# Attention values with the exponentials as stationary operand, a ones column for the sums, and a turn by TensorE

## Chip, cores, metric

One core of one Trainium2 chip. The metric is the device time of one execution in microseconds, lower is better.

## The reference, cut to what matters

Attention over 8 batches, 8 heads, 576 queries, 16 beacon keys and 576 causal keys, head size 64, followed by a gated feed-forward block (512 to 1536 to 512) on the 4608 tokens.

```python
k_all = np.concatenate([beacon_k, k], axis=2)          # 592 keys
v_all = np.concatenate([beacon_v, v], axis=2)
scores = scale * q @ k_all.T                           # causal mask on the 576
a = np.exp(scores - max); a /= a.sum(-1) + 1e-9
x = (a @ v_all) -> (B*S, H*D)
out = (gelu(x @ w_gate) * (x @ w_val)) @ w_out
# ... cut
```

## The kernel before

Heads are worked in pairs (four pairs per batch), keys in five tiles t of up to 128. Scores are computed as keys by queries, so the exponentials expT have keys on partitions. Only the causal part is computed: it is packed in four chunks. Each chunk has its scores in one of **two** PSUM buffers (`psum_s`), from which ScalarE takes the exponential into `expT`; GpSimd (in batch 0 VectorE) masks the diagonal afterwards.

```python
CHUNK_W = [512, 480, 464, 208]           # columns of a chunk, for each of two heads
psum_s = tile_pool(name="psum_s", bufs=2, space=PSUM)    # scores, gate/value: 2 x 2 banks
psum_x = tile_pool(name="psum_x", bufs=1, space=PSUM)    # x and sums: 3 banks
psum_o = tile_pool(name="psum_o", bufs=1, space=PSUM)    # output matmuls: 1 bank

def scores(b, m, c):
    s_ps = psum_s.tile([P, 2, 512], FP32, tag="s")
    ...                                   # matmuls of 64 rows, two heads side by side
    act(expT[:, :, o : o + w], s_ps[:, :, 0:w], ACT.Exp, scale=QK_SCALE)
    if b: masks(b, m, c)

def attend(b, m, t, wide=False):          # V or ones stationary, expT moving
    for w, (ps, base, split) in enumerate(x_of[i]):       # w = 0: x, w = 1: the sums
        for q0, q1 in ((S_LO[t], split), (max(split, S_LO[t]), S)):
            for hi in range(2):           # two heads in two 64-column tiles of TensorE
                mm(ps[64*hi : 64*hi+64, base+q0 : base+q1],
                   ones[0:kr, :] if w else v_sb[0:kr, t, 2*m+hi, :],
                   expT[0:kr, hi, e0 : e0 + q1 - q0], ...)

def normalize(b, m, ...):                 # ... cut: the sums stand in all 64 partitions
    act(x_sb, x_ps, ACT.Copy)
    nc.vector.transpose(zT_sb, z_ps)
    nc.vector.reciprocal(r_sb, ...)       # 18 values after the 32x32 transpose
    nc.vector.transpose(rec_sb, r_sb broadcast)
    nc.vector.tensor_tensor(out=xT_sb[...], in0=x_sb, in1=rec_sb, op=mult)
```

In batches 1 to 7 the output matmuls of the previous batch, `o(n)`, are spread between the pairs. `ab` computes two chunks, `cd` the other two, `av` is attend and normalize:

```python
o(6); ab(0); o(10); cd(0); o(8)
for m in range(1, NPAIR):
    ab(m); av(m - 1); cd(m); o(6 if m < NPAIR - 1 else 5)
av(3, direct=True); o(7)
# then 12 x gate_val(b, fi): 8 matmuls of 512 columns each
```

Batch 0 has no previous batch and runs its value matmuls at the end of its attention.

The softmax here doesn't subtract the row's maximum and nothing guards it: scores larger than these inputs give would overflow.

## Time and profile before

| | before |
|---|---|
| median time | 398.38 us (397.85 to 398.61), 398.12 with the fourth run |
| span of the profiled run | 396.2 us |
| TensorE, ScalarE, VectorE busy | 97%, 51%, 48% |
| length of a batch (first scores to first scores of the next) | 42.18 us |
| distance of two pairs within a batch | 4.03 us |

The groups below, from the list of costliest groups, are those that the change removes (line, engine, operation, tile names, shapes, count | busy us, mean ns | idle before).

```profile
L155 PE MATMUL x_ps<-expT,ones 128*64 128x432 bf16 (+1 forms) x558 | 41.2, 243 | 0.0
L304 DVE STREAM_TRANSPOSE zT_sb<-x_ps 128x576 f32<-128x576 f32 x29 | 22.7, 781 | 29.9 <-ACT x_sb L158 29.9
L307 DVE STREAM_TRANSPOSE rec_sb<-r_sb 128x576 f32<-128x576 f32 x29 | 22.6, 778 | 1.0
```

Busy time of TensorE here counts pipelined matmuls one over the other, so 41.2 us of the ones matmuls isn't 41.2 us of span, and "busy" also covers short waits.

### The profile page before, as it was taken

What the parts mean: (1) busy time and instruction counts of PE and PEld (TensorE: products, weight loads), DVE (VectorE), ACT (ScalarE), POOL (GpSimd) and SP (SyncE); (2) the same over time, 40 slices, a digit from 0 to 9 for tenths busy, and PEclk for the clock granted to TensorE, in tenths of its full rate; (3) what the DMA queues carried; (4) which work ended last, traced back from release to release, by engine and by line L of the source; (5) the groups of instructions that cost most, each with busy time, mean ns of one, the idle gap of its engine ahead of it and who ended that gap; (6) DMA issues with size and microseconds to landing.
All of it is one profiled execution on the core that took longest, in us unless ns stands there. A gap on an engine that the chain in (4) does not pass through costs nothing.

```text
span 396.2 us, 7413 instructions
## 1 busy us (share of the span) xinstructions
PE 382.3 (97%) x3046; PEld 185.9 (47%) x3046; DVE 190.5 (48%) x304; ACT 202.2 (51%) x280; POOL 156.3 (39%) x277
## 2 busy tenths in 40 slices
PE   3889999999999999999999999999999999999996
PEld 2464545544454445444544455444544455444442
DVE  1393654844375327642673338433754266332332
ACT  2775258634873379336843586347823793332210
POOL 8722395780369124931486047803400240000000
PEclk9999999999999999999999999999999999999999
DMA  7999998699129930996099915991032010000012
GB/s 91 180 206 204 175 132 97 68 169 121 55 36 156 141 79 30 120 156 84 29 107 162 89 55 57 163 137 58 28 89 59 34 45 32 0 0 29 28 53 106
DMA packets 139154, 36.24 MB, mean 91 GB/s; under 512 B 126832, under 2 KB 134512, under 8 KB 139120
## 3 DMA queue, kind: packets, MB, share of 16 engines
q0 software_dynamic: 103984, 19.14, 64.4%
q1 hardware_dynamic: 35136, 16.62, 19.3%
q8 instruction: 24, 0.39, 0.4%
q14 instruction: 10, 0.08, 0.1%
HBM read 38.27 MB, written 9.44 MB: 120 GB/s over the span
## 4 chain that ended last, share of the span: by engine, by line
PE 79%; DMA 8%; POOL 3%; DVE 3%; ACT 3%; issue 2%; SPq 2%; POOLq 0%; ACTq 0%
PE gv_ps L155 36%; PE o_ps L155 23%; PE x_ps L155 11%; PE s_ps L155 8%; DMA qkT<-k_sb_94 3%; DMA v_sb_98<-in_beacon_v_dram 2%; SPq L196 2%; ACT expT L158 2%; DMA k_sb_97<-in_k_dram 2%; POOL k_sb_97 L109 1%; PE t_ps L167 1%; DVE qkT L178 1%; POOL q_sb_96 L109 1%; PE w_ps L155 1%; DMA kb<-in_beacon_k_dram 1%
## 5 line engine op out<-in xcount | busy, mean ns | idle before, releaser
L158 ACT ACTIVATE ge_sb<-gv_ps 128x512 bf16<-128x512 f32 x108 | 64.5, 597 | 150.7 <-PE gv_ps L155 150.7
L340 DVE TENSOR_TENSOR hT_sb<-gv_ps,ge_sb 128x512 bf16<-128x512 f32 x108 | 74.7, 692 | 116.0 <-ACT ge_sb L158 116.0
L158 ACT ACTIVATE expT<-s_ps 128x1024 bf16<-128x1024 f32 (+3 forms) x128 | 103.9, 870 | 25.8 <-PE s_ps L155 25.7
L155 PE MATMUL gv_ps<-xT_sb,wg_sb 128*128 128x512 bf16 x432 | 112.2, 379 | 0.8 <-DVE xT_sb L312 0.8
L155 PE MATMUL gv_ps<-xT_sb,wv_sb 128*128 128x512 bf16 x432 | 112.2, 379 | 0.0
L238 POOL TENSOR_SCALAR_AFFINE_SELECT expT<-expT 128x256 bf16<-128x256 bf16 (+2 forms) x140 | 52.4, 388 | 142.2 <-ACT expT L158 142.1
L155 PE MATMUL o_ps<-wo_sb,hT_sb 128*128 128x512 bf16 x432 | 103.6, 380 | 0.0
L155 PEld LDWEIGHTS <-wv_sb 128*128 128x128 bf16 x432 | 42.3, 98 | 52.7 <-issue 2.7
L155 PEld LDWEIGHTS <-wg_sb 128*128 128x128 bf16 x432 | 41.9, 98 | 49.9
L155 PEld LDWEIGHTS <-hT_sb 128*128 128x128 bf16 x432 | 38.8, 98 | 46.6 <-issue 2.8
L364 DVE COPY o_sb<-o_ps 128x512 f32<-128x512 f32 x36 | 24.7, 687 | 37.9 <-PE o_ps L155 37.9
L155 PE MATMUL s_ps<-qkT 64*128 64x80 bf16 (+5 forms) x384 | 39.1, 294 | 2.7 <-DVE qkT L183 1.5
L155 PE MATMUL x_ps<-expT,ones 128*64 128x432 bf16 (+1 forms) x558 | 41.2, 243 | 0.0
L304 DVE STREAM_TRANSPOSE zT_sb<-x_ps 128x576 f32<-128x576 f32 x29 | 22.7, 781 | 29.9 <-ACT x_sb L158 29.9
L155 PEld LDWEIGHTS <-qkT 64*128 64x128 bf16 x384 | 14.8, 96 | 30.4 <-issue 21.8
L155 PEld LDWEIGHTS <-ones 128*64 128x64 bf16 (+1 forms) x578 | 23.2, 110 | 4.6
L307 DVE STREAM_TRANSPOSE rec_sb<-r_sb 128x576 f32<-128x576 f32 x29 | 22.6, 778 | 1.0
L155 PE MATMUL x_ps<-expT,v_sb_95 128*64 128x80 bf16 (+5 forms) x270 | 21.5, 245 | 1.5 <-DVE zT_sb L304 1.1
L155 PE MATMUL x_ps<-expT,v_sb_98 128*64 128x80 bf16 (+5 forms) x288 | 22.8, 246 | 0.0
L109 POOL DMA_DIRECT2D v_sb_98<-in_v_dram x20 | 17.0, 868 | 11.9 <-DMA wv_sb<-in_moe_w_val_dram 3.7
L109 POOL DMA_DIRECT2D v_sb_95<-in_v_dram x20 | 17.0, 889 | 2.5 <-DMA k_sb_94<-in_k_dram 2.3
L312 DVE TENSOR_TENSOR xT_sb<-x_sb,rec_sb 128x576 bf16<-128x576 f32 x23 | 17.4, 758 | 0.9
(51 smaller groups left out, 190.9 us busy)
## 6 DMA issues: line engine op xcount, KB each, us to landing
out_dram<-o_sb SPq DMA_DIRECT2D x36, 256.0 KB, 2.0
v_sb_95<-in_v_dram POOLq DMA_DIRECT2D x12, 128.0 KB, 7.9
wg_sb<-in_moe_w_gate_dram POOLq DMA_DIRECT2D x3, 512.0 KB, 11.6
wv_sb<-in_moe_w_val_dram POOLq DMA_DIRECT2D x3, 512.0 KB, 13.3
wo_sb<-in_moe_w_out_dram POOLq DMA_DIRECT2D x1, 1536.0 KB, 23.5
v_sb_98<-in_v_dram POOLq DMA_DIRECT2D x12, 128.0 KB, 10.6
q_sb_93<-in_q_dram POOLq DMA_DIRECT2D x12, 128.0 KB, 4.2
q_sb_96<-in_q_dram POOLq DMA_DIRECT2D x12, 128.0 KB, 4.2
```

The costliest lines, as they stand in the source:

```text
L109: keep(nc.gpsimd.dma_start(out=out_ap, in_=in_ap))
L155: keep(nc.tensor.matmul(out_ap, lhsT, rhs, start=start, stop=stop, **kw))
L158: keep(nc.scalar.activation(out_ap, in_ap, func, **kw))
L167: keep(nc.tensor.transpose(out_ap, in_ap, ident[0:n, 0:n]))
L178: nc.vector.tensor_copy(qkT[:, m, :, NB:SK].rearrange("p w (t r) -> p w t r", r=6), t_ps[:, 0:2, 0:S].rearrange("p w (r t) -> p w t r", r=6),)
L196: nc.sync.dma_start_transpose(out=qkT[:, :, w, c + j * P : c + j * P + n], in_=src[0:n, j, :, :].rearrange("p h d -> p (h d)"),)
L238: nc.gpsimd.affine_select(out=d, in_=d, pattern=[[0, 2], [1, n]], compare_op=ALU.is_ge, fill=0.0, base=NB if t == 0 else 0, channel_multip ...
L304: keep(nc.vector.transpose(zT_sb, z_ps))
L307: nc.vector.transpose(rec_sb.rearrange("p (c o) -> p c o", o=32), r_sb.to_broadcast([P, S // 32, 32]))
L312: nc.vector.tensor_tensor(out=xT_sb[:, m, b * S : (b + 1) * S], in0=x_sb, in1=rec_sb, op=ALU.mult)
L340: nc.vector.tensor_tensor(out=h_of[ci][:, fi, :], in0=gv_ps[:, 1, :], in1=ge_sb, op=ALU.mult)
L364: keep(nc.vector.tensor_copy(o_sb[:, ti, :], o_ps))
```

## The change

The roles are exchanged: 128 queries' exponentials are the stationary operand, 64 value columns and one column of ones are the moving one. The result has queries on partitions, with each query's sum in the 65th column, so that normalizing is a reciprocal and a multiply per partition. TensorE then transposes the result into the layout that the gate matmuls need ("turn"). The intent: 36 matmuls become 30 short ones, the ones matmuls and the two stream transposes go, and ScalarE loses its copy of x. The chunks are now computed in the order 0, 2, 1, 3; "third" and "fourth chunk" below mean the third and fourth in time.

```diff
-AV_ORDER = [0, 2, 4, 1, 3]
+AB, CD = (0, 2), (1, 3)          # chunks 0 and 2 first, then 1 and 3
+DV = D + 1
+Q_LO = [0, 112, 240, 368, 448]
+SLOT = [0, 2 * DV, 4 * DV, 512, 512 + 2 * DV]
+    psum_t = ctx.enter_context(tc.tile_pool(name="psum_t", bufs=1, space=PSUM))
-        vt = ring.tile([P, 5, H, D], ...)
+        vt = ring.tile([P, 5, H, DV + 1], ...); memset(vt[:, :, :, D:], 1.0)
     def attend(b, m, wide=False):
+        for j in range(5):
+            for hi in range(2):
+                c0 = SLOT[j] + hi * DV
+                for t in range(j + 1):
+                    mm(x_ps[:, c0 : c0 + DV],
+                       expT[0 : KROWS[t], hi, e0 : e0 + P],
+                       v_sb[0 : KROWS[t], t, 2 * m + hi, 0:DV], t == 0, t == j)
     def normalize(b, m):
+        for c0, j0, n in ((0, 0, 6), (512, 6, 4)):
+            nc.vector.reciprocal(r, x[:, :, D:DV])
+            nc.vector.tensor_tensor(out=y_sb[...], in0=x[:, :, 0:D], in1=r broadcast, op=mult)
+    def turn(b, m):
+        y_ps = psum_t.tile([P, 1024], BF16, tag="t")
+        for j in (4, 3, 2, 1, 0):
+            nc.tensor.transpose(y_ps[...], y_sb[0:n, j, :], ident[0:n, 0:n])
+        nc.vector.tensor_copy(xT_sb[:, m, b * S : (b + 1) * S], y_ps[:, 0:S])
     # batches 1 to 7
             for m in range(1, NPAIR):
                 ab(m); av(m - 1); cd(m); o(6 if m < NPAIR - 1 else 5)
+                turn(b, m - 1)
-            av(3, direct=True); o(7)
+            av(3); o(7)
+            turn(b, 3)
     # batch 0
-            av(1, by_act=True); av(2, wide=True, ...); av(3, ...)
+            av(1); av(2, wide=True); turn(b, 0); turn(b, 1); av(3); turn(b, 2); turn(b, 3)
     # ... cut
```

## The prediction

> **What bounds the kernel now.** I read the head of the page first, then the chain that ended last, then one head pair of the attention stage in the timeline, because the change touches that stage alone.
>
> ```profile
> span 396.2 us, 7413 instructions
> PE 382.3 (97%) x3046; PEld 185.9 (47%) x3046; DVE 190.5 (48%) x304; ACT 202.2 (51%) x280; POOL 156.3 (39%) x277
> ...
> PE 79%; DMA 8%; POOL 3%; DVE 3%; ACT 3%; issue 2%; SPq 2%; POOLq 0%; ACTq 0%
> PE gv_ps L155 36%; PE o_ps L155 23%; PE x_ps L155 11%; PE s_ps L155 8%; DMA qkT<-k_sb_94 3%; DMA v_sb_98<-in_beacon_v_dram 2%; SPq L196 2%; ACT expT L158 2%; DMA k_sb_97<-in_k_dram 2%; POOL k_sb_97 L109 1%; PE t_ps L167 1%; DVE qkT L178 1%; POOL q_sb_96 L109 1%; PE w_ps L155 1%; DMA kb<-in_beacon_k_dram 1%
> ```
>
> TensorE is busy 97% of the span and owns 79% of the chain; the matmuls that the change rewrites (x_ps, values and sums) hold 11% of it, so at first sight each microsecond saved there counts. The timeline of one pair (batch 2, its second pair: start, us, engine, line, operation, count) corrects that:
>
> ```profile
> 103.69 0.60 PE L155 MATMUL s_ps<-qkT 64*128 64x512 bf16 x8
> ...
> 104.18 1.89 ACT L158 ACTIVATE expT<-s_ps 128x1024 bf16<-128x1024 f32 x2 [0.95 <-PE s_ps L155]
> ...
> 105.78 0.60 PE L155 MATMUL s_ps<-qkT 64*128 64x464 bf16 x4
> 105.95 0.66 ACT L158 ACTIVATE x_sb<-x_ps 128x576 f32<-128x576 f32 x1
> ...
> 106.32 1.47 PE L155 MATMUL o_ps<-wo_sb,hT_sb 128*128 128x512 bf16 x6
> ...
> 107.72 0.60 PE L155 MATMUL s_ps<-qkT 64*128 64x512 bf16 x8
> ```
>
> A pair takes 107.72 - 103.69 = 4.03 us. Its second score group, at 105.78, looks like solid work, but its columns (464 and 208) need only about 0.28 us of streaming and the next matmuls come 0.54 us later. The start times of single instructions in the trace say why: the matmul of the fourth chunk (208 columns) starts at 106.120, 51 ns after the second exponential ends (106.069). It needs that exponential's PSUM buffer, as there are only two score buffers. This 50 ns spacing recurs in every later pair of batches 1 to 7, except the first one of each. So the pair stands on a round trip: scores, two exponentials on ScalarE, then the fourth chunk's scores, 2.43 us after the pair began. The value matmuls lie wholly inside it.
>
> **What the skill says, and whether this trace agrees.**
> (1) "TensorE: Matmul & The Clock Gate", section on weight-path perf modes: Fast Weight Load is on for 128 weight columns that are not fp32. The trace agrees in direction: loads of 128 columns take 96 to 98 ns, those of 64 columns 110 ns.
> (2) The same page, back-to-back issue gap: N/2.4 + 2.5 ns alone, but about 81 ns per matmul at N = 128 in a sustained stream of load and matmul. Here the trace sides with the first: 64 columns with a fresh 128-column stationary are followed after 28 ns, 80 columns with fresh 64-column weights after 40 ns, 512 columns after 216 ns.
> (3) "TensorEngine Tiling (Array Packing)", key properties: changing the tiling mode drains TensorE. In this trace each change of tile shape costs about 0.1 us beyond the streaming (o_ps to s_ps, s_ps to x_ps, x_ps to s_ps, s_ps to o_ps).
> (4) The clock page again, part on the HAM clock gate: TensorE falls back to half clock after an idle window of about 3.4 us. No stretch of this trace tests that after the start; the first 512-column score matmuls of the run took about 605 ns against 386 later.
>
> **The change part by part.**
> *Value matmuls.* Before: 36 per pair, 1.56 us with the drain. After: for each of 5 query blocks and 2 heads, 1 to 5 key tiles, 30 matmuls of 65 columns. At 65/2.4 + 2.5 = 29.6 ns (estimate from point 2 and its 28 ns) that is 0.89 us: 0.67 us less.
> *Turn, added.* 5 transposes of 128 columns at about 56 ns (same formula): 0.28 us per pair on TensorE, as 128-column tiles without a drain to o_ps. A PSUM copy of 128x576 on VectorE is added: 0.75 us at most (from the 687 ns of the 512-column copy).
> *VectorE.* Removed per pair: two stream transposes of 0.78, a reciprocal of 0.27, a multiply of 0.76: 2.6 us with gaps. Added: two short reciprocals (0.2 each with gaps), multiplies of 384 and 256 elements (estimates 0.56 and 0.43: this trace has 692 ns for 512 elements and 758 for 576, about 1 ns an element), and the copy: about 2.2 us. Never the bound in steady state.
> *ScalarE.* It loses the 0.66 us copy of x (22 times). That copy follows the exponential that TensorE waits for, so it isn't in the round trip.
> *Order of chunks.* The first two become 512 and 464 columns instead of 512 and 480: about 0.03 us less exponential in the round trip.
>
> Now the sum, for a pair in the middle, from its first score matmul: first exponential at +0.495, second at about +1.41, its end at about +2.36, the fourth chunk at 2.41 (before 2.43). The value matmuls end at about 1.41 and the third chunk at about 1.78, then TensorE **waits about 0.6 us** instead of 0.14. After that 0.20 (chunk and drain), six o_ps matmuls of 0.216 = 1.30, the turn 0.28, a drain 0.10: period 4.28 against 4.03. The saving has gone into the wait; the turn is paid in full: **+0.25 us**, for two pairs of each of 7 batches. At a batch's end, from the third of these pairs to the gate matmuls: saved there 0.67 and two drains beside the last value group (0.2), since these are now full tiles; paid two turns, 0.56, a wait of about 0.2 as the last turn comes after 1.5 us of o_ps while reciprocals and multiplies need about 1.7 after the last value matmul. Adding the step from the fourth chunk on: 15.43 us from the second pair to the gate stage against 14.95, less about 0.11 of waiting that the gate matmuls had on the last xT slice: **+0.37 us per batch** in all, 2.6 us for seven.
>
> *Batch 0* has no other work to hide in. Before, gate matmuls began at 29.6 and its four postponed ones at 31.95, so it acted like a start at 30.66. After, normalisation and turns run through one psum_t buffer and VectorE in this order: the first normalise after the masks, 23.3 to 24.7; second value group to 25.6, normalise to 27.3; third to 28.7; copy of turn 0 to 29.4; turn 1 and its copy to 30.7; fourth normalise (value group only at 29.8 to 30.7) to 32.3; copy 2 to 33.0; turn 3 until 33.3, when the gate matmuls start. That is **+2.7 us**.
>
> Relief: batches 4 and 6 waited 0.2 to 0.3 us for DMA transposes into qkT (their first pair's fourth chunk came 624 and 724 ns after the last exponential, against 397 elsewhere); the longer batch end gives back perhaps 0.3 in all. Sum: 2.6 + 2.7 - 0.3 = 5.0 us on 398.4, thus about 403.5.
>
> **Rivals.**
> *The saving is real.* If the round trip didn't bind, each of 28 later pairs would gain 0.67 - 0.28 = 0.39 us, 11 us, and with batch 0 the time would be about 390. For it: TensorE is shown busy throughout. Against: the 50 ns rule above, which busy figures hide.
> *Short matmuls are slow.* At 81 ns a group would take 2.4 us; then two middle pairs per batch overrun the wait by 0.9 each, and the last value group costs 1.5 more: some 23 us, thus about 426. Against: the 28 and 40 ns of this trace, though no row has 128 rows, 128 columns and so short a stream at once. At an intermediate 50 ns (1.5 us) only the last group and batch 0 pay, +6 us.
> *Batch 0 cools TensorE.* TensorE would idle for 2.7 and 2.0 us there, short of the window of point 4 but with little work between. Being throttled would cost perhaps 2 to 3 us more. I give it a third, and it shifts the range upward.
> *VectorE or the DMA transposes become the bound.* Against: about 2.9 us of VectorE work per pair with the o_sb copies against 4.3; the loads that precede qkT come no later.
>
> **Range and chances.** The mechanism is well supported for 21 pairs, so the time hangs on the batch ends and on batch 0. Low end 399.5: batch 0 loses 1 us, turns half hidden. High end 409: throttled start, 40 ns matmuls. Below 390.4 needs the round trip not to bind: 4%. Above 406.4 needs one of the upward rivals: 21%.
>
> **What the new profile would show.** Right: x_ps matmuls 30 ns apart; each fourth chunk still about 50 ns after the second exponential, with some 0.6 us of TensorE idle before it; middle pairs 4.2 to 4.3 us apart; gate matmuls of batch 0 beginning near 33.3 with xT copies of turns on the chain; ScalarE without x_sb. Wrong, if pairs come closer than 4.0 us, if x_ps takes over 1.4 us, or if batch 0 ends no later than before.

## The result, and the profile after

| | before | after |
|---|---|---|
| median time | 398.12 us (397.68 to 398.61) | 401.49 us (400.59 to 403.2) |
| span of the profiled run | 396.2 us | 398.9 us |
| length of a batch | 42.18 us | 42.45 us |
| distance of two middle pairs | 4.03 us | 4.28 us |
| batch 0: first value matmul to first output matmul | 33.89 us | 34.91 us |

The ratio is 1.009, 95% interval 1.0063 to 1.0117. A ratio is the mean time of one kernel's fast runs over that of the other's of the same rounds, so it isn't quite the ratio of the medians. The change makes the kernel 0.9% slower.

The head of the page of the changed kernel, its chain by engine, and the new groups:

```profile
span 398.9 us, 7336 instructions
PE 368.8 (92%) x2960; PEld 186.1 (47%) x3010; DVE 168.1 (42%) x345; ACT 186.2 (47%) x252; POOL 155.5 (39%) x277
...
PE 81%; ACT 10%; DVE 4%; issue 2%; DMA 1%; POOL 0%; ACTq 0%; POOLq 0%; DVEq 0%
...
L156 PE MATMUL x_ps<-v_sb,expT 128*128 128x65 bf16 x930 | 33.6, 193 | 0.6 <-DVE y_sb L289 0.6
...
L300 DVE COPY xT_sb<-y_ps 128x576 bf16<-128x576 bf16 x32 | 14.5, 453 | 19.0 <-PE y_ps L299 19.0
...
L299 PE MATMUL y_ps<-ident,y_sb 128*128 128x128 bf16 (+1 forms) x160 | 14.1, 218 | 3.4 <-DVE xT_sb L300 3.4
```

Every engine that was to be relieved is less busy, TensorE too (part of its fall is missing records: the trace holds 414 of 432 gate matmuls and 403 of 432 output matmuls). But the time is longer, and **ScalarE has appeared in the chain with 10%**: in the kernel before it had 3%. The timeline of one middle pair shows the place (TensorE and ScalarE alone):

```profile
105.33 0.59 PE L156 MATMUL s_ps<-qkT 64*128 64x512 bf16 x4
...
105.82 3.13 ACT L159 ACTIVATE expT<-s_ps 128x1024 bf16<-128x1024 f32 x4 [0.93 <-PE s_ps L156]
105.85 1.09 PE L156 MATMUL x_ps<-v_sb,expT 128*128 128x65 bf16 x30
...
106.89 0.38 PE L156 MATMUL s_ps<-qkT 64*128 64x64 bf16 x6
...
107.73 0.27 PE L156 MATMUL s_ps<-qkT 64*128 64x208 bf16 x2 [0.45 <-ACT expT L159]
...
107.93 1.47 PE L156 MATMUL o_ps<-wo_sb,hT_sb 128*128 128x512 bf16 x5
109.23 0.44 PE L299 MATMUL y_ps<-ident,y_sb 128*128 128x128 bf16 x5
109.60 0.58 PE L156 MATMUL s_ps<-qkT 64*128 64x512 bf16 x4
```

The 30 value matmuls start 30.7 ns apart on average (105.847 to 106.738 in the trace's start times) and are done early. The fourth chunk (64x208) then waits for an exponential: 0.45 us by the view, which subtracts modelled pipeline ends, and 0.61 us by start times and columns (the last matmul of the third chunk has 80 columns, 34 ns at the rate at which 512 take 216 ns, and the wait is counted from there). It starts 51 to 52 ns after the second exponential ends, in the second to fourth pair of every batch from 1 to 7. The turn at 109.23 then stands alone ahead of the next pair.

### The profile page after: what moved, and what is told of

Its sections match the earlier page's. It is cut to its first block, busy times and chain, and to the rows that moved or that the text cites. A ratio compares the mean times of both kernels' runs of the same rounds, so it can differ in the third digit from the quotient of the medians.

```text
span 398.9 us, 7336 instructions
## 1 busy us (share of the span) xinstructions
PE 368.8 (92%) x2960; PEld 186.1 (47%) x3010; DVE 168.1 (42%) x345; ACT 186.2 (47%) x252; POOL 155.5 (39%) x277
## 4 chain that ended last, share of the span: by engine, by line
PE 81%; ACT 10%; DVE 4%; issue 2%; DMA 1%; POOL 0%; ACTq 0%; POOLq 0%; DVEq 0%
PE gv_ps L156 46%; PE o_ps L156 24%; ACT expT L159 10%; PE s_ps L156 6%; PE y_ps L299 2%; PE x_ps L156 2%; PE t_ps L168 1%; DVE y_sb L289 1%; DVE qkT L179 1%; DMA kb<-in_beacon_k_dram 1%; DVE expT L236 1%; PE w_ps L156 0%; DVE hT_sb L325 0%; ACT ge_sb L159 0%; POOL qk L110 0%
## 5 line engine op out<-in xcount | busy, mean ns | idle before, releaser
L156 PE MATMUL s_ps<-qkT 64*128 64x336 bf16 (+5 forms) x384 | 39.4, 290 | 13.0 <-ACT expT L159 11.3
L110 POOL DMA_DIRECT2D v_sb<-in_v_dram x40 | 33.8, 862 | 14.0 <-DMA wv_sb<-in_moe_w_val_dram 3.6
L156 PEld LDWEIGHTS <-expT 128*128 128x128 bf16 (+1 forms) x960 | 31.1, 97 | 9.6 <-POOL expT L239 8.5
L156 PE MATMUL x_ps<-v_sb,expT 128*128 128x65 bf16 x930 | 33.6, 193 | 0.6 <-DVE y_sb L289 0.6
L289 DVE TENSOR_TENSOR y_sb<-x_ps,r_sb 128x384 bf16<-128x384 f32 (+1 forms) x62 | 30.4, 491 | 2.1
L156 PEld LDWEIGHTS <-qkT 64*128 64x128 bf16 x384 | 15.1, 95 | 30.8 <-issue 22.3
L110 POOL DMA_DIRECT2D q_sb<-in_q_dram x30 | 25.3, 855 | 6.1 <-DMA wo_sb<-in_moe_w_out_dram 6.1
L110 POOL DMA_DIRECT2D k_sb<-in_k_dram x30 | 25.4, 891 | 0.0
L300 DVE COPY xT_sb<-y_ps 128x576 bf16<-128x576 bf16 x32 | 14.5, 453 | 19.0 <-PE y_ps L299 19.0
L287 DVE RECIPROCAL r_sb<-x_ps 128x6 f32<-128x6 f32 (+1 forms) x62 | 11.4, 184 | 22.7 <-PE x_ps L156 22.7
L299 PE MATMUL y_ps<-ident,y_sb 128*128 128x128 bf16 (+1 forms) x160 | 14.1, 218 | 3.4 <-DVE xT_sb L300 3.4
```

Source lines behind the costliest of these rows:

```text
L110: keep(nc.gpsimd.dma_start(out=out_ap, in_=in_ap))
L156: keep(nc.tensor.matmul(out_ap, lhsT, rhs, start=start, stop=stop, **kw))
L287: keep(nc.vector.reciprocal(r, x[:, :, D:DV]))
L289: nc.vector.tensor_tensor(out=y_sb[:, j0 : j0 + n, :], in0=x[:, :, 0:D], in1=r.to_broadcast([P, n, D]), op=ALU.mult)
L299: keep(nc.tensor.transpose(y_ps[:, Q_LO[j] : Q_LO[j] + n], y_sb[0:n, j, :], ident[0:n, 0:n]))
L300: keep(nc.vector.tensor_copy(xT_sb[:, m, b * S : (b + 1) * S], y_ps[:, 0:S]))
```

## The experiments

Two theories. **The round trip:** between the first scores of a pair and its fourth chunk stand two exponentials; TensorE can't pass this point earlier, so work moved into that stretch is free and work outside is paid. **Its rival, TensorE's own work:** TensorE is nearly always busy, so the sum of its matmuls sets the time, and the change is slower because turns and short matmuls cost more than they save.

The length of a batch is read from the traces, first scores to first scores of the next. It is steady to 0.01 or 0.02 us in most batches (batch 1 is up to 0.18 us shorter, a few others are up to about 1 us longer; the length quoted is that of the rest), while the times scatter more, for a reason that comes below. The changed kernel was run again beside the others:

> The changed kernel again, on the chip of the runs beside it: 0.7 to 1.2% slower than before (401 to 402.5 us), middle pairs 4.28 us apart. Both theories expect this; it is the reference for the others. The mean clock of its profile shows whether batch 0 cooled TensorE in this run.

Measured: median of the five fast runs 400.61 us, ratio 1.0087 (1.0046 to 1.0127). Its profiled run was slow (mean clock 0.951 over the whole run) and isn't used. So the profile of the first measurement stays the reference.

### The turn moved into the wait

```diff
                 ab(m)
+                if m > 1:
+                    turn(b, m - 2)
                 av(m - 1)
                 cd(m)
                 o(6 if m < NPAIR - 1 else 5)
-                turn(b, m - 1)
+            turn(b, 2)
             av(3)
```

> The turn of a pair is issued one pair later, between the first score group and the value matmuls, thus inside the stretch in which TensorE waits. Theory (the round trip scores - two exponentials - fourth chunk binds): the turn becomes free in the second and third of these pairs, their distance falls from 4.28 to about 4.0 us, time falls by 14 x 0.28 = 3.9 us to about 397.5, near before. Rival (TensorE's own work binds, its wait is no slack): no change, 401.5, since the same instructions run.

Measured: 396.76 us, ratio 0.9981 (0.9952 to 1.001); batches 41.90 us against 42.45, thus 0.55 less where 0.56 was expected. A middle pair of this run, TensorE alone in the timeline:

```profile
107.73 0.58 PE L156 MATMUL s_ps<-qkT 64*128 64x512 bf16 x4
108.24 0.45 PE L299 MATMUL y_ps<-ident,y_sb 128*128 128x128 bf16 x5
108.53 1.07 PE L156 MATMUL x_ps<-v_sb,expT 128*128 128x65 bf16 x30
...
110.13 0.27 PE L156 MATMUL s_ps<-qkT 64*128 64x208 bf16 x2 [0.21 <-ACT expT L159]
...
111.73 0.58 PE L156 MATMUL s_ps<-qkT 64*128 64x512 bf16 x4
```

The same matmuls run, the wait is shorter by the turn (0.37 us instead of 0.61 by start times), and pairs are 4.00 us apart instead of 4.28. The rival expected no change, so it falls. The interval includes equality with the kernel before: one reordering gives back what the change lost.

### Value matmuls made longer, inside and outside

For one head of the pair, the 15 value matmuls are run twice, with the same result; first in the three value groups inside round trips, then in the last group of each batch alone.

```diff
-        for j in range(5):
-            for hi in range(2):
+        for j, hi in [(j, hi) for j in range(5) for hi in range(2)] + [(j, 0) for j in range(5) if pad]:
```

> 15 of the 30 value matmuls are run twice (same result) in the three value groups of each batch that lie inside the round trip, 0.45 us each. Theory: they fill part of the 0.6 us wait and cost nothing, under 1 us in all; the gap ahead of the fourth chunk falls from about 0.63 to 0.18 us. Rival (TensorE issue binds): 21 x 0.45 = 9.4 us slower than the changed kernel, about 411.

> 15 of the 30 value matmuls run twice in the last value group of each batch alone, which lies outside any round trip. Theory: 0.45 us is paid in each of 7 batches, 3.1 us slower than the changed kernel, about 404.5. Rival (value matmuls are hidden anywhere): no change.

Measured inside: 401.76 us, ratio 1.0103 (1.0068 to 1.0138); batches 42.60 us, 0.15 longer for 3 x 0.45 = 1.35 us of added matmuls (1.05 us in seven batches, where under 1 was expected). The wait ahead of the fourth chunk fell to 0.19 us, and middle pairs stayed 4.28 us apart. The 0.15 us stand at the end of the batch: in the last value group, which isn't padded, there is one gap of 0.17 us, which ends 57 ns after GpSimd's mask; that mask comes later because the third chunk does. Outside: 403.79 us, ratio 1.0137 (1.0116 to 1.0158); batches 42.90, 0.45 longer for 0.45 added, all of it paid. The time rose by 2.3 to 3.2 us, by the fast medians of the two measurements of the changed kernel, where 3.1 was expected; the batches rose by exactly that. So inside, the length of the value matmuls is almost free, and a saving there buys almost nothing. That is where the expected gain went.

### ScalarE made longer, inside and outside

```diff
         act(expT[:, :, o : o + w], s_ps[:, :, 0:w], ACT.Exp, scale=QK_SCALE)
+        if b and m and c == 0:            # inside; outside: c == 1
+            junk = npool.tile([P, 2, 208], BF16, name="junk", tag="junk")
+            act(junk, s_ps[:, :, 0:208], ACT.Exp, scale=QK_SCALE)
```

> An extra exponential of 416 columns to a scratch tile after the first exponential of the second to fourth pair of batches 1 to 7, thus inside the round trip. Theory: about 0.45 us each, 21 x 0.45 = 9.4 us slower than the changed kernel, near 411, with the fourth chunk still about 50 ns behind the second exponential. Rival (ScalarE is not on the path, busy 47%): no change.

> The same extra exponential after the third one, outside the round trip. Theory: no change against the changed kernel, within 1 us (the buffers come free at about 3.7 and 4.2 us of a pair of 4.28). Rival (total work of ScalarE per pair counts): about as slow as the run with it inside.

Measured inside: 409.68 us, ratio 1.0286 (1.0261 to 1.031); batches 43.68 us, 1.23 longer, 0.41 for each extra exponential (about 0.45 was put down), with the fourth chunk still 50 to 51 ns behind the second exponential. Outside: 401.85 us, ratio 1.009 (1.0069 to 1.011), the same ratio as the changed kernel without it; batches 42.61. The same instruction costs 0.41 us in one place and about 0.05 in the other. The timeline of the run with it inside has both waits:

```profile
107.51 0.38 PE L156 MATMUL s_ps<-qkT 64*128 64x64 bf16 x6 [0.37 <-ACT junk L159]
108.35 0.27 PE L156 MATMUL s_ps<-qkT 64*128 64x208 bf16 x2 [0.45 <-ACT expT L159]
```

ScalarE is busy for less than half of the span, and still 0.4 us of it costs 0.4 us where it stands between scores and scores.

### Output matmuls moved into the wait

```diff
                 av(m - 1)
+                o(3)
                 cd(m)
-                o(6 if m < NPAIR - 1 else 5)
+                o(3 if m < NPAIR - 1 else 2)
                 turn(b, m - 1)
```

> Three o_ps matmuls of each of the three pairs move from behind the second score group to right behind the value matmuls, inside the round trip. Theory: 3 x 0.216 us of work goes into the wait, pairs come 3.7 to 3.9 us apart, 21 x 0.4 = about 8 us less than the changed kernel, near 393, unless the third chunk, now later, starves ScalarE. Rival (nothing but the sum of TensorE's work counts): no change, 401.5.

Measured: 397.3 us, ratio 0.9996 (0.9971 to 1.002); batches 41.90. Better by 0.55 us per batch, but less than half of what was expected. The pairs did come closer (3.63 and 3.82 us). The gain was given back at the end of the batch, in the last value group:

```profile
117.98 0.41 PE L156 MATMUL x_ps<-v_sb,expT 128*128 128x65 bf16 x8
...
118.78 0.39 PE L156 MATMUL x_ps<-v_sb,expT 128*128 128x65 bf16 x7 [0.38 <-POOL expT L239]
...
119.41 0.63 PE L156 MATMUL x_ps<-v_sb,expT 128*128 128x65 bf16 x15 [0.25 <-POOL expT L239]
```

With both last chunks computed later, their exponentials and then GpSimd's masks come later, and the value matmuls of the last pair, which have only two output matmuls ahead of them now, wait twice for masks (each time the next matmul starts 57 ns after a mask ends): 1.89 us for the group instead of 0.91. Here moved work has turned into a new wait.

The same edit on the kernel before:

> The kernel before with three o_ps matmuls moved behind the value matmuls, the edit of the fill run. Theory (the slack of 0.6 us was made by the change; before it there was 0.14): no gain, 0 to 1% slower than before, as the second score group now comes after the exponentials are done and ScalarE starves. Rival (the slack was there before too and the reordering alone brings the gain): about 9 us faster, 389.

Measured: 405.54 us, ratio 1.019 (1.0173 to 1.0207): 1.9% slower, more than the 0 to 1% expected. Pairs are 4.25 and 4.44 us apart (from 4.03). The timeline of one pair (TensorE and ScalarE alone):

```profile
105.37 1.89 ACT L158 ACTIVATE expT<-s_ps 128x1024 bf16<-128x1024 f32 x2 [0.95 <-PE s_ps L155]
...
107.14 0.66 ACT L158 ACTIVATE x_sb<-x_ps 128x576 f32<-128x576 f32 x1
107.72 0.46 PE L155 MATMUL s_ps<-qkT 64*128 64x464 bf16 x4
...
108.13 1.35 ACT L158 ACTIVATE expT<-s_ps 128x928 bf16<-128x928 f32 x2 [0.33 <-PE s_ps L155]
109.12 0.76 PE L155 MATMUL s_ps<-qkT 64*128 64x512 bf16 x6 [0.19 <-ACT expT L158]
```

With the longer value matmuls the second score group comes 0.47 us after the second exponential has ended. ScalarE has only its copy of x to do meanwhile and then idles for 0.33 us. The next pair's first scores start 52 ns after the late third exponential, for whose buffer they wait, and the scores of its second chunk 52 ns after the fourth. So the slack that this edit uses is one that the change made. The reordering isn't good by itself.

### Batch 0

The prediction put +2.7 us on batch 0; the trace has +1.02. Its timeline in the changed kernel (TensorE and VectorE alone):

```profile
28.10 0.45 DVE L300 COPY xT_sb<-y_ps 128x576 bf16<-128x576 bf16 x1
28.60 0.45 PE L299 MATMUL y_ps<-ident,y_sb 128*128 128x128 bf16 x5 [1.92 <-DVE xT_sb L300]
28.89 1.08 PE L156 MATMUL x_ps<-v_sb,expT 128*128 128x65 bf16 x30
...
31.27 0.45 DVE L300 COPY xT_sb<-y_ps 128x576 bf16<-128x576 bf16 x1
...
31.77 0.44 PE L299 MATMUL y_ps<-ident,y_sb 128*128 128x128 bf16 x5 [1.53 <-DVE xT_sb L300]
```

TensorE waits 1.92 and 1.53 us for VectorE to empty the single turn buffer. The copy itself takes 0.45 us; before it VectorE has normalizing to do. The experiment removes this: the last value group goes into the second score buffer, the turns alternate between two PSUM buffers, and ScalarE, idle there, does the copies.

```diff
-            av(1); av(2, wide=True); turn(b, 0); turn(b, 1); av(3); turn(b, 2); turn(b, 3)
+            av(1); av(2, wide=True); av(3, wide=True)
+            for m in range(NPAIR):
+                turn(b, m, alt=True)      # odd m: PSUM tile of psum_o; copy by nc.scalar
-    npool = ... bufs=2
+    npool = ... bufs=4
```

> Batch 0 alone: third and fourth value groups in both score buffers, the turns alternate between two PSUM buffers, their copies run on ScalarE. Theory (VectorE's order and the single turn buffer delay batch 0): gate matmuls begin near 30 instead of 32 us, 1.5 to 2.3 us less than the changed kernel. Rival (batch 0 waits for something else, such as loads): no change. All profiles and times: if cooling of TensorE makes the runs scatter, they scatter less here.

Measured: 398.74 us, ratio 1.0009 (0.9989 to 1.0029). From its first value matmul to the first output matmul batch 0 takes 33.08 us instead of 34.91, 1.83 less, within what was expected. The time fell by 1.9 to 2.8 us by the fast medians. The edit changes the buffers and the engine of the copies at once, so it doesn't say what each is worth.

**Cooling.** Of the 46 fast runs of kernels that keep the batch 0 of the change, 10 had a mean clock of 0.996 or less and were about 1 to 5 us longer than the others of the same kernel. None of 33 runs of the kernel before beside them did (0.998 or more), none of 6 with the new batch 0 alone, one of 5 of the final version below, which has the new batch 0 too. Four of the 10 runs were profiled: the clock was halved within batch 0 for 6.8 us in three and for 3.4 us in one (the padded last group, mean clock 0.996). In stretches of 3 us of the run with the padded inner groups (stretch: us, then busy us of TensorE, weight loads, VectorE, ScalarE and GpSimd, granted clock, DMA share, GB/s):

```profile
24.00:27.00 3.00, 1.76 (x47) 1.66 (x46) 2.65 (x12) 2.34 (x3) 0.67 (x2) 0.89 1.24 206
27.00:30.00 3.00, 1.57 (x25) 1.32 (x22) 2.32 (x8) 0.00 (x0) 0.83 (x1) 0.50 1.25 209
30.00:33.00 3.00, 2.86 (x40) 2.62 (x40) 0.98 (x4) 0.00 (x0) 0.88 (x1) 0.50 1.29 202
```

The 0.50 is a half clock. Batch 0 took 37.14 us there, 2.2 more than the 34.91 of a run that stayed at full clock. About 0.65 of this is not the clock, by an estimate from the ends of the masks: they came 2.54 us after the fourth pair's first scores in this run and 1.89 in the other. The padding leaves batch 0 as the change made it, so this belongs to the change, in some of its runs. The profiles show one difference: TensorE's gap ahead of the second value group was 1.31 to 1.50 us in the four runs with a halved clock, where the masks came late, and 0.85 to 0.98 in the four other fast profiles with this batch 0. The gap alone doesn't decide, since the kernel before had 1.36 there and the run with the new batch 0 had 1.29, both at full clock; but they have more work behind it (from 27 to 30 us TensorE is busy for 2.62 and 2.35 us, in the changed kernel for 1.40). That the late masks together with the light load halve the clock fits these counts and was not tested.

### A version that follows from the runs

```diff
                 ab(m)
+                if m > 1:
+                    turn(b, m - 2)
                 av(m - 1)
-                cd(m)
-                o(6 if m < NPAIR - 1 else 5)
-                turn(b, m - 1)
+                n = 3 - m                 # 2, 1, 0
+                scores(b, m, CD[0])
+                o(n)
+                scores(b, m, CD[1])
+                o((6 if m < NPAIR - 1 else 5) - n)
+            turn(b, 2)
             av(3)
```

The third chunk's scores go first, so that ScalarE is fed, then output matmuls fill the wait, and the last pair isn't delayed. The first run has the new batch 0 as well, the second hasn't.

> All that the runs so far point to, on the changed kernel: turns one pair later inside the round trip, two o_ps matmuls (second pair) and one (third pair) between the third and the fourth chunk's scores so that ScalarE is fed first, none in the last pair so that the masks ahead of the last value group aren't delayed, and the batch 0 of the earlier run. Theory: batches 41.3 us long (42.45 in the changed kernel, 41.9 with turns early), batch 0 shorter by 1.8 us: about 390 us, 2% under before. Rival (moved work returns as another wait, as in the fill run): batches stay at 41.9, about 395.5.

> The same as the first of this call without the change to batch 0. Theory: batches 41.3 us long, about 392 to 393 us, with some of its runs 3 to 5 us longer at a mean clock of 0.99 (TensorE cooled in batch 0), which the first of this call should not have. Rival: batches 41.9, 397.

Measured with the new batch 0: **391.08 us, ratio 0.9822 (0.9803 to 0.9841)** against the kernel before, the best of all; half of its batches 41.32 us, as expected, the others up to 0.5 longer in the profiled run. Without it: 394.18 us, ratio 0.9889 (0.9867 to 0.9911), batches 41.32, and its profiled run (395.1 us) was one of those with the cooled batch 0 (mean clock 0.991, 37.12 us there). The 394.18 is more than the 392 to 393 expected, and only one of its six runs was cooled; where the rest went isn't known. With its freed time used, the changed kernel is 1.8% faster than the kernel before. Whether the kernel before would gain from the smaller moves of this version was not run; the record has only the move of three output matmuls, which made it slower.

## Why the prediction was right, point by point

The prediction was right: 401.49 us lies within 399.5 to 409, near the 403.5 given, and "within 2%" had the 75% that its 4% and 21% leave.

- **Short matmuls.** 29.6 ns each was the estimate, 30.7 ns measured. Right. (One reading under it is partly off: 40 ns after 80 columns is the case of 80 rows; with 128 rows the same trace has 35.) The rival of 81 ns per matmul is out.
- **The round trip.** The fourth chunk was to start about 50 ns after the second exponential; it is 51 to 52 ns. The wait was to grow from 0.14 to 0.6 us; it is 0.61. Pairs were to be 4.28 us apart; they are. The four experiments with work added inside and outside show that this is the cause, not only a coincidence of numbers.
- **The turn paid in full.** Right: moving it inside gave back 0.55 us of an expected 0.56 per batch.
- **A whole batch.** +0.37 us per batch was put down, +0.27 measured. The difference is at the batch end: the wait for the last turn is 0.1 us, not 0.2.
- **Batch 0, the term that was mis-sized.** "+2.7 us" measured +1.0. The gate matmuls were to begin near 33.3; the first one in the trace starts at 32.27. Two parts of that row of times were too long. The copies of turns were put at 0.75 us "at most" from an fp32 copy; they take 0.45, and two of them stand on the chain. This bf16 copy took 453 ns for 576 elements, the fp32 one 691 for 512. The Trainium skill, "VectorE: DVE Perf Modes", the errata section's cycle table, would have come near: 120 + FD/Accel cycles for a copy from PSUM, at two elements per cycle, gives an estimate of 425 ns. (It doesn't fit every bf16 copy: the one of 1152 elements into qkT, with a rearranged output, took 1353 ns.) And the masks ahead of the first normalize ended 1.9 us after the fourth pair's first scores instead of 2.4. This part is luck of the run: over the profiles with this batch 0 it is 1.9 to 2.5, and 1.9 in the second profile with the old one. Together the two are about 1.1 of the 1.7 us; the rest wasn't taken apart.
- **The relief.** The batches that were longer in the kernel before, 42.41 and 42.50 us instead of 42.18, take 42.45 and 42.43 like all others: 0.55 us less beyond the common difference, where 0.3 was put down. This is luck of the profile and not shown to be the change's doing: in other runs with the same attention one or two of these batches are longer again, by 0.1 to 0.9 us (42.73 in the run with the new batch 0 alone, 42.88 and 43.54 with the extra exponential outside).
- **Sum of the profiled runs:** 0.4 (value matmuls of batch 0 begin later, at 21.73 instead of 21.36, before anything that the change slows; this start moved between 20.5 and 22.3 us in the experiments, so it is luck too) + 1.0 + 7 x 0.27 - 0.55 = 2.7 us, which is 398.9 - 396.2.
- **Cooling** was a rival at one third. It happened in 10 of 46 runs, and these are the runs farthest up in the scatter. A cost of 2 to 3 us was put down; batch 0 was 2.2 us longer in the three runs with 6.8 us of half clock.

## What to carry to other kernels

An engine that reads as 97% busy can still be waiting. Compare the start of a matmul with the end of what frees its buffer, and where the same small distance recurs (here 50 ns), that buffer's round trip sets the pace. A saving inside such a stretch brought almost nothing here until work from outside was moved into it, and the work must be moved such that the engine on the other side of the round trip is still fed first. Check also what stands at the end of the stage, since later masks or copies take the gain back.

## What the Trainium skill lacked or had wrong

- "TensorE: Matmul & The Clock Gate", back-to-back issue gap: its sustained figures for streams of load and matmul, about 81 ns at 128 columns and 131 at 512, don't hold here. With a fresh 128-column stationary each, the transposes of a turn (128 columns) ran 56 ns apart, the output matmuls (512) 216, and the value matmuls (65) 30.7, all near the formula N/2.4 + 2.5 that it gives for the isolated case.
- The same page, part on the HAM clock gate: its table has the clock fall after an idle window of about 3.4 us. Here it was halved in batch 0 for 6.8 or 3.4 us although the longest gap between TensorE starts in the 5 us before was 1.36 to 1.50 us in three runs and 2.13 in one; at full clock the changed kernel had gaps of 2.13 us as well. The page also names short idle times between groups of matmuls as a cause, but has no length or share for them.
- "TensorEngine Tiling (Array Packing)", key properties: it says that a change of mode drains TensorE, without a figure. Here a change cost about 0.1 us, four times per pair; from turn to value matmuls, both full tiles, the next start came 54 ns after the last one of 112 columns, thus without a drain.
- "Perfetto Trace Analysis", Identifying the Most-Contended Engine, says that matmul busy time is no good measure, since matmuls are pipelined. It doesn't say that waits can hide in it: a pair of the kernel before shows TensorE busy for 4.03 of 4.03 us with a wait of 0.14 us inside.
